# Value tiles loaded by natural rows, weights in 1 KB runs, and a replanned order table, in a local attention with attention experts behind it

## The chip, the cores and the metric

The kernel runs on one core of one Trainium2 chip. The metric is the device time of one execution in microseconds, as the median of several executions. Beside it there is a profile of one execution; its span runs from the first to the last instruction. The engines are named as in the profile: PE is TensorE's matmuls and PEld its weight loads, DVE is VectorE, ACT is ScalarE, POOL is GpSimd, SP is SyncE, which here only issues transfers. ACT issues some transfers too, between its own work. Every engine works through its instructions in order.

## The reference

There are two stages. The first is attention with a local window of 96 keys and 8 global keys, for 4 batches, 8 heads, 768 positions and 64 numbers per head. The second takes the first's output, with the heads side by side (512 numbers per position), through four causal attention experts; a gate picks two of the four for each position.

```python
# first stage: q, k, v are [4, 8, 768, 64] float32
scores = scale * np.matmul(q, k.transpose(0, 1, 3, 2))
rel = pos[:, None] - pos[None, :]
keep = (pos[None, :] < n_global) | ((rel >= 0) & (rel < n_local))
scores = np.where(keep, scores - slopes[h] * dist, -1e9)
a = np.exp(scores - max); a /= a.sum(-1)
attn = np.matmul(a, v)                       # [4, 8, 768, 64]
x = attn.transpose(0, 2, 1, 3).reshape(4, 768, 512)

# second stage: w_gate [512, 4], wq, wk, wv [4, 512, 64], wo [4, 64, 512]
logits = x @ w_gate                          # softmax over the best two of four
for e in range(4):
    q, k, v = x @ wq[e], x @ wk[e], x @ wv[e]
    a = softmax(causal(scale * q @ k.T))
    out += gate_weight[e] * (a @ v @ wo[e])  # [4, 768, 512] float32
```

## The kernel before

The work is cut into 24 units `u`, each a row tile of 128 positions of one batch (six for each batch). For each unit there is a set of small stages, and a long table, `ORDER`, lists the stages in the order in which they are given to the engines. A slot of the table is two letters for the stage, the number of the unit, and a letter for the engine: `g` POOL, `a` ACT, `v` DVE for copies and casts, `s` SP and `a` ACT for transfers. So `lq0s` loads tile 0 of the queries on SP's queue, `qc0g` casts it to 16 bits on POOL, `tk0` and `tq0a` turn keys and queries on PE and copy the result on ACT, `sa0` and `sb0` are tile 0's local scores with their exponential on ACT, `gs` the global scores, `vs` the selected global values, `va` and `vb` the local values, `tx` turns x, `pk`, `pq` and `pv` project it, `ca`, `cb` and `cc` are the causal scores, `ma` their mask on POOL, `za` and `zb` the causal values, `tz` and `ou` the output, `ro` the routing, `wi` and `wc` load and cast weights. `xb`, `xg` and `az` fill constants on DVE.

Keys and queries are loaded by row tile, with the positions on the partitions. For the values, the local stage wants another layout: 64 keys on 64 partitions, heads 0 to 3 on the lower half of the partitions and heads 4 to 7 on the upper half. The kernel before loads them from memory in that layout, so that one cast for each unit is enough:

```python
raw = fast.enter_context(tc.tile_pool(name="raw", bufs=4))

def load(u, nm, on):
    b, ri = divmod(u, NT)
    f = fs[nm, u] = raw.tile([P, H, Dh], F32, name=nm + "f")
    queues[on](f[:, :, :], {"k": k, "q": q}[nm][b, :, ri * P:(ri + 1) * P, :]
               .rearrange("h j d -> j h d"))

def load_v(i, on):
    if i < 2:                                # tiles 0 and 1 of the first batch alone
        parts = [(hf, slice(0, HG), 2 * i + c) for hf in range(2) for c in range(2)]
        b = 0
    else:                                    # one head of each half, all the batch's rows
        b, hq = divmod(i - 2, HG)
        parts = [(hf, hq, slice(0 if b else 4, 2 * NT)) for hf in range(2)]
    if i == 0 or i > HG + 1 and hq == 0:
        fs["v", b] = raw.tile([P, HG, 2 * NT, Dh], F32, name="vf", bufs=2)
    for hf, h, c in parts:
        o, r = fs["v", b][hf * KB:(hf + 1) * KB], v[b, hf * HG:(hf + 1) * HG]
        if i < 2:
            queues[on](o[:, :, c, :], r[:, c * KB:(c + 1) * KB, :].rearrange("h j d -> j h d"))
        else:
            queues[on](o[:, h, c, :], r[h, c.start * KB:c.stop * KB, :]
                       .rearrange("(c j) d -> j c d", j=KB))

def cast_v(u, on):
    b, ri = divmod(u, NT)
    copies[on](take("vbuf", u)[:, :, :, 0:Dh],
               fs["v", b][:, :, 2 * ri:2 * ri + 2, :].rearrange("r h c d -> r c h d"))
```

The weights of keys, queries and values are loaded with position `kp` of 128 on the partition and four chunks `ko` behind each other, which makes pieces of 256 bytes; the gate's weights make pieces of 16 bytes.

```python
def weights_in(i, on):
    w32s[i] = wst.tile([P, E, NK, Hd], F32, name="w32", tag="w32")
    issue = queues[on]
    if i < 3:
        issue(w32s[i][:, :, :, :],
              (moe_wk, moe_wq, moe_wv)[i].rearrange("e (ko kp) d -> kp e ko d", kp=P))
    else:
        ...                                  # wo
    if i == 2:
        w32s["g"] = wst.tile([P, NK, E], F32, name="wg32", tag="wg32", bufs=1)
        issue(w32s["g"][:, :, :], moe_w_gate.rearrange("(ko kp) e -> kp ko e", kp=P))

def turn_x(u, on):
    x_ps = psT.tile([P, NK, P], F16, name="xps", tag="t")
    for j in range(NK):
        nc.tensor.transpose(x_ps[:, j, :],
                            x16s[u][:, j // 2, 2 * (j % 2):2 * (j % 2) + 2, :]
                            .rearrange("r h d -> r (h d)"), ident[:, :])
    xTs[u] = pp.tile([P, NK, P], F16, name="xT")
    copies[on](xTs[u][:, :, :], x_ps[:, :, :])
```

The beginning of its order table:

```
az0 lq0s xb0 lk0s qc0g kc0g tk0 lv0a lk1a vc0g lq1s lk2s kc1g lk3s lq2a lq3s lq4a xg0 tq0a lk4s
tk1 qc1g tq1v wi0a kc2a gi0 kc3v vs0 lv1s sa0 tk2 lq5s qc2g tq2v tk3 lk5a az1 az2 az3 sb0 qc3g
tq3v az4 gs0 vg0 qc4g kc4g lq6s tk4 lv2s wi1a tq4v lk6a sa1 sa2 va0 vb0 sb1 sa3 lv3s kc5v vc1g
lv4s lv5a vg1 va1 vb1 qc5g qc6g sb2 lk7s tk5 tq5v lq7s wc0g wi2a lk8a lk9s tx0v tx1v wc1g kc6v
sa4 sa5 pk0 pk1 lq8s pq0v vc2g vc3v vc4g pq1v vc5g sb3 vg2 gs1 tk6 kc7v lv6s va2 ca0 vb2 lq9a
...
```

Of the kernel before, what the change touches and what calls it, by code (L numbers as in the profile page):

```python
# [22 lines left out]
def kernel(  # L23
# [120 lines left out]
    def weights_in(i, on):  # L144

        w32s[i] = wst.tile([P, E, NK, Hd], F32, name="w32", tag="w32")
        issue = queues[on]
        if i < 3:
            issue(w32s[i][:, :, :, :],
                  (moe_wk, moe_wq, moe_wv)[i].rearrange("e (ko kp) d -> kp e ko d", kp=P))  # L150
        else:
            issue(w32s[i][:, :, :, :].rearrange("p e k d -> p (e k d)")
                  .rearrange("p (a m) -> p a m", a=NEP),
                  moe_wo.rearrange("(a b) d m -> (b d) a m", b=2))
        if i == 2:
            w32s["g"] = wst.tile([P, NK, E], F32, name="wg32", tag="wg32", bufs=1)
            issue(w32s["g"][:, :, :], moe_w_gate.rearrange("(ko kp) e -> kp ko e", kp=P))  # L157

    def weights_cast(i, on):
# [6 lines left out]
        elif i == 2:  # L166
# [3 lines left out]
            copy(wvg16[:, :, E * Hd:E * Hd + E], w32s["g"][:, :, :])  # L170
# [8 lines left out]
    raw = fast.enter_context(tc.tile_pool(name="raw", bufs=4))  # L179
# [8 lines left out]
    NA, NV, NV2 = 5, 8, 2 * NT + 2  # L188
    rings = {}
# [34 lines left out]
    def load(u, nm, on):  # L224
        b, ri = divmod(u, NT)
        f = fs[nm, u] = raw.tile([P, H, Dh], F32, name=nm + "f")
        queues[on](f[:, :, :], {"k": k, "q": q}[nm][b, :, ri * P:(ri + 1) * P, :]
                   .rearrange("h j d -> j h d"))

    def load_v(i, on):  # L230

        if i < 2:
            parts = [(hf, slice(0, HG), 2 * i + c) for hf in range(2) for c in range(2)]
            b = 0
        else:
            b, hq = divmod(i - 2, HG)
            parts = [(hf, hq, slice(0 if b else 4, 2 * NT)) for hf in range(2)]
        if i == 0 or i > HG + 1 and hq == 0:  # L240
            fs["v", b] = raw.tile([P, HG, 2 * NT, Dh], F32, name="vf", bufs=2)
        for hf, h, c in parts:
            o, r = fs["v", b][hf * KB:(hf + 1) * KB], v[b, hf * HG:(hf + 1) * HG]
            if i < 2:
                queues[on](o[:, :, c, :], r[:, c * KB:(c + 1) * KB, :].rearrange("h j d -> j h d"))
            else:
                queues[on](o[:, h, c, :], r[h, c.start * KB:c.stop * KB, :]  # L247
                           .rearrange("(c j) d -> j c d", j=KB))
# [8 lines left out]
    def cast_v(u, on):  # L257
        b, ri = divmod(u, NT)
        copies[on](take("vbuf", u)[:, :, :, 0:Dh],  # L259
                   fs["v", b][:, :, 2 * ri:2 * ri + 2, :].rearrange("r h c d -> r c h d"))  # L260
# [41 lines left out]
    def global_scores(g):  # L302

        u0 = g * NH
        b, r0 = divmod(u0, NT)
        kg = kgs[b]
        g_ps = psS.tile([P, NH * P], F32, name="gps", tag="s")
# [3 lines left out]
        for p in range(NP):  # L311
            for c0, c1 in (((0, P), (P, NH * P)) if r0 == 0 else ((0, NH * P),)):
# [4 lines left out]
        ag = pp.tile([P, NH * P], F16, name="ag", bufs=3)  # L317
        S_.activation(ag[:, :], g_ps[:, :], func=Exp, bias=gbias[:, :], scale=sc1)
        ags[g] = ag
# [29 lines left out]
    def global_values(u):  # L349

        c = (u % NT % NH) * P
        ag, vg = ags[u // NH], vgs[u // NT]
        zs_[u] = psZ.tile([P, 2, 4 * P], F32, name="zps", tag="z")
        for hf in range(2):
            r = slice(hf * Dh, hf * Dh + Dh)
            mm(zs_[u][:, hf, 0:HG * VW].rearrange("r (h d) -> r h d", h=HG),  # L356
               lhsT=ag[r, c:c + P], rhs=vg[r, :, :],
# [25 lines left out]
    def turn_x(u, on):  # L383
        x_ps = psT.tile([P, NK, P], F16, name="xps", tag="t")
        for j in range(NK):
            nc.tensor.transpose(x_ps[:, j, :],  # L386
                                x16s[u][:, j // 2, 2 * (j % 2):2 * (j % 2) + 2, :]
                                .rearrange("r h d -> r (h d)"), ident[:, :])
# [75 lines left out]
    def causal_values(u, i):  # L464
# [4 lines left out]
        if i == 0:  # L469
            zs2[u] = psZ.tile([P, 2, 4 * P], F32, name="zps2", tag="z")  # L470
# [71 lines left out]
    def general_path(ctx):  # L542
# [35 lines left out]

        ident32 = gc.tile([P, P], F32, name="ident32")
# [20 lines left out]
        with tc.For_i(0, B, 1) as b:  # L600
# [43 lines left out]
            for ri in range(NT):  # L644
                l_ps = gp.tile([P, MAXB], F32, name="gs", tag="s", bufs=2)
                for ko in range(NK):
                    mm(l_ps[:, 0:E], lhsT=xT[:, ko, ri * P:(ri + 1) * P],
                       rhs=wvg16[:, ko, E * Hd:E * Hd + E],
# [6 lines left out]
            for e in range(E):  # L655
                for w, dst, nm in ((wq16, qs, "q"), (wk16, ks, "k")):
                    d = gb.tile([Hd, S], F16, name=f"g{nm}T{e}")
                    for c in range(2):
                        p_ps = gp.tile([P, MAXB], F32, name="gs", tag="s", bufs=2)
                        for ko in range(NK):  # L660
                            mm(p_ps[0:Hd, 0:S // 2], lhsT=w[:, ko, e // 2, e % 2, :],
# [6 lines left out]
                for ct in range(NT):  # L668
                    p_ps = gp.tile([P, MAXB], F32, name="gs", tag="s", bufs=2)
                    for ko in range(NK):  # L670
                        mm(p_ps[:, 0:Hd], lhsT=xT[:, ko, ct * P:(ct + 1) * P],
                           rhs=wvg16[:, ko, e * Hd:(e + 1) * Hd],
# [41 lines left out]
        "lk": (load, "k"), "lq": (load, "q"), "lv": (load_v,),  # L714
# [3 lines left out]
        "az": (local_zeros,), "xt": (act_tables,),  # L718
# [40 lines left out]

ORDER = """  # L760
az0 lq0s xb0 lk0s qc0g kc0g tk0 lv0a lk1a vc0g lq1s lk2s kc1g lk3s lq2a lq3s lq4a xg0 tq0a lk4s
tk1 qc1g tq1v wi0a kc2a gi0 kc3v vs0 lv1s sa0 tk2 lq5s qc2g tq2v tk3 lk5a az1 az2 az3 sb0 qc3g
tq3v az4 gs0 vg0 qc4g kc4g lq6s tk4 lv2s wi1a tq4v lk6a sa1 sa2 va0 vb0 sb1 sa3 lv3s kc5v vc1g
lv4s lv5a vg1 va1 vb1 qc5g qc6g sb2 lk7s tk5 tq5v lq7s wc0g wi2a lk8a lk9s tx0v tx1v wc1g kc6v
sa4 sa5 pk0 pk1 lq8s pq0v vc2g vc3v vc4g pq1v vc5g sb3 vg2 gs1 tk6 kc7v lv6s va2 ca0 vb2 lq9a
tq6v sb4 sb5 lk10s lk11a qc7g wc2g tk7 tq7v vg3 va3 tx2v kc8g vb3 kc9v sa6 sb6 lv7s pv0v pv1a
vg4 va4 qc8g qc9g vb4 lv8a lv9s pk2 pq2a tk8 tq8v kc10v lk12s ca1 lk13a vg5 lq10s lq11s va5
tx3v lq12s tk9 tq9v gi1 gs2 tx4v vb5 pv2a pv3a sa7 sa8 tx5v ma0 pk3 ro0 vc6g ro0 vc7v vc8v pq3a
# [68 lines left out]
```

## Time and profile before

| | before |
|---|---|
| time, median of 3 | 161.3 us (161.09 to 161.34) |
| span of the profiled execution | 160.6 us |
| PE busy | 134.7 us (84%) |
| DVE, ACT busy | 112.0 us (70%), 105.4 us (66%) |
| POOL busy | 71.1 us (44%) |
| moved by transfers | 27.80 MB, 173 GB/s over the span |
| packets under 512 B | 82256 of 85623 |

A busy share is an average over the whole span. The page also cuts the span into 40 slices and gives each engine a digit for each slice, in tenths. The chain of waits follows the work that ended last back to the start: at each step, to what released it. The groups of instructions give the count, the busy time and the mean time of one for each line and shape; behind the second bar stands how long the engine stood idle before them and what it waited for.

### The profile page before, as it was taken

How to read it: one execution, taken by the hardware profiler on the slowest of the kernel's cores; microseconds unless marked ns; L12 is line 12 of the kernel's file. 1: busy time of each engine (PE TensorE's matmuls, PEld its weight loads, DVE VectorE, ACT ScalarE, POOL GpSimd, SP SyncE). 2: the span in 40 equal slices, each digit the busy share in tenths (PEclk: the TensorE clock that was granted, in tenths of full speed). 3: DMA queues.
4: the chain of work that ended last, by engine and by line, in shares of the span. 5: the costliest groups of instructions: out<-in, count | busy, mean ns of one | idle time of the engine just before them, and what ended most of it. 6: DMA issues, size and time to landing. Idle time of an engine off the chain costs nothing.

```text
span 160.6 us, 6996 instructions
## 1 busy us (share of the span) xinstructions
PE 134.7 (84%) x2950; PEld 105.8 (66%) x2950; DVE 112.0 (70%) x343; ACT 105.4 (66%) x171; POOL 71.1 (44%) x187
## 2 busy tenths in 40 slices
PE   0266585779999999899999999999999999999710
PEld 0143363758778879787798876887889778776300
DVE  7978424248769977597796588788866788798530
ACT  0283051074648878788968988989878788799520
POOL 4454343093308463976636643603435254633100
PEclk9999558778999999999999999999999999999995
DMA  5999998999999989795499999032100103042550
GB/s 115 273 288 257 260 236 180 270 257 224 241 256 247 255 189 284 169 225 140 126 227 232 228 293 251 33 131 76 65 6 0 69 6 135 0 172 93 200 208 8
DMA packets 85623, 27.80 MB, mean 173 GB/s; under 512 B 82256, under 2 KB 82256, under 8 KB 85584
## 3 DMA queue, kind: packets, MB, share of 16 engines
q1 hardware_dynamic: 64480, 21.63, 53.6%
q10 hardware_dynamic: 21104, 5.65, 15.8%
q8 instruction: 25, 0.41, 1.1%
q14 instruction: 14, 0.11, 0.2%
HBM read 20.98 MB, written 6.29 MB: 170 GB/s over the span
## 4 chain that ended last, share of the span: by engine, by line
PE 60%; DMA 16%; ACTq 5%; SPq 4%; DVE 3%; ACT 2%; issue 2%; POOL 2%; POOLq 0%
DMA vf<-in_v_dram 11%; PE pps L401 11%; PE vps L415 7%; PE cps L446 6%; PE zps L371 6%; PE tp L267 6%; PE zps L474 5%; PE ops L502 4%; PE sps L334 4%; PE xps L386 4%; SPq L247 3%; DMA kf<-in_k_dram 3%; PE sps L341 3%; ACTq L157 3%; PE zps L356 2%; DMA out_dram<-osb 2%
## 5 line engine op out<-in xcount | busy, mean ns | idle before, releaser
L449 ACT ACTIVATE a<-cps 128x1024 f16<-128x1024 f32 (+1 forms) x48 | 42.0, 915 | 5.7 <-PE cps L446 5.1
L344 ACT ACTIVATE abuf<-sps 128x636 f16<-128x636 f32 (+1 forms) x48 | 30.7, 684 | 20.3 <-PE sps L341 8.5
L259 POOL CAST vbuf<-vf 128x512 f16<-128x512 f32 x20 | 12.3, 637 | 20.5 <-DMA vf<-in_v_dram 9.9
L334 PE MATMUL sps<-biasT,ident 64*64 64x318 f16 (+1 forms) x192 | 16.0, 333 | 5.8 <-ACT abuf L344 5.8
L461 POOL TENSOR_SCALAR_AFFINE_SELECT a<-a 128x256 f16<-128x256 f16 x48 | 18.5, 415 | 5.2 <-ACT a L449 5.2
L276 DVE COPY kqT<-tp 128x1024 f16<-128x1024 f16 x22 | 15.0, 685 | 6.1 <-PE tp L267 5.9
L267 PE MATMUL tp<-ident,s16k 128*128 128x128 f16 x96 | 10.5, 239 | 8.6 <-POOL s16k L255 8.1
L380 DVE TENSOR_TENSOR x<-zps,rinv 128x512 f16<-128x512 f32 x24 | 16.6, 691 | 0.8
L255 POOL CAST s16q<-qf 128x512 f16<-128x512 f32 x21 | 12.9, 622 | 8.6 <-DMA qf<-in_q_dram 5.7
L371 PE MATMUL zps<-vbuf,abuf 64*128 64x65 f16 x704 | 16.7, 195 | 0.0
L341 PE MATMUL sps<-kqT 64*64 64x159 f16 (+2 forms) x384 | 15.6, 243 | 0.8 <-issue 0.7
L371 PEld LDWEIGHTS <-abuf 64*128 64x128 f16 x704 | 15.2, 98 | 1.1 <-issue 0.4
L401 PE MATMUL pps<-xT,wk 128*128 128x128 f16 x192 | 15.4, 227 | 0.0
L474 PE MATMUL zps<-v2buf,a 128*128 128x65 f16 x336 | 15.3, 193 | 0.0
L401 PE MATMUL pps<-xT,wq 128*128 128x128 f16 x192 | 14.9, 223 | 0.0
L474 PEld LDWEIGHTS <-a 128*128 128x128 f16 x336 | 12.9, 97 | 1.7 <-DVE zs L485 0.2
L502 PE MATMUL ops<-wo,zt 128*128 128x512 f16 x48 | 13.5, 380 | 0.4 <-DVE zt L495 0.4
L341 PEld LDWEIGHTS <-kqT 64*64 64x64 f16 x384 | 12.3, 116 | 2.4 <-issue 1.4
L415 PE MATMUL vps<-wvg,xT 128*128 128x260 f16 x96 | 13.7, 274 | 0.0
L267 PEld LDWEIGHTS <-s16k 128*128 128x128 f16 x96 | 6.6, 106 | 10.6 <-POOL s16k L255 8.3
L446 PEld LDWEIGHTS <-kq 64*128 64x128 f16 x336 | 9.7, 94 | 4.9 <-issue 3.8
L446 PE MATMUL cps<-kq,kq 64*128 64x128 f16 x240 | 12.9, 217 | 0.0
(111 smaller groups left out, 267.5 us busy)
## 6 DMA issues: line engine op xcount, KB each, us to landing
out_dram<-osb SPq DMA_DIRECT2D x24, 256.0 KB, 2.3
qf<-in_q_dram SPq DMA_DIRECT2D x20, 256.0 KB, 4.8
kf<-in_k_dram SPq DMA_DIRECT2D x18, 256.0 KB, 4.9
vf<-in_v_dram SPq DMA_DIRECT2D x22, 192.0 KB, 4.4
kf<-in_k_dram ACTq DMA_DIRECT2D x6, 256.0 KB, 5.2
qf<-in_q_dram ACTq DMA_DIRECT2D x4, 256.0 KB, 5.3
vf<-in_v_dram SPq DMA_DIRECT2D x6, 128.0 KB, 6.5
w<-in_moe_wk_dram ACTq DMA_DIRECT2D x1, 512.0 KB, 6.7
```

Of the source, the lines that this page charges most:

```text
L267: nc.tensor.transpose(tps[u][:, i, p, :], s16s["kq"[i], u][:, 2 * p:2 * p + 2, :].rearrange("j h d -> j (h d)"), ident[:, :])
L334: mm(s_ps[o, hh, 0:2 * w].rearrange("r (c n) -> r c n", c=2), lhsT=ident2[r, :], rhs=biasT[r, p, 0:w].unsqueeze(1).to_broadcast([KB, 2, w] ...
L341: mm(s_ps[o, hh, c * w:c * w + n], lhsT=kqT[b][r, 0, p, k0:k0 + KB], rhs=kqT[b][r, 1, p, k0:k0 + n], start=False, stop=True, skip_group_ch ...
L344: S_.activation(as_[u][:, :, g, :].rearrange("r h (c n) -> r h c n", c=2)[:, :, :, 0:w], s_ps[:, :, 0:2 * w].rearrange("r h (c n) -> r h c ...
L371: mm(zs_[u][:, hf, hq * VW:(hq + 1) * VW], lhsT=as_[u - prev][r, hq % 2, hq // 2, at:at + P], rhs=held("vbuf", u - prev)[r, c, hq, :], sta ...
L401: mm(p_ps[:, i, ep, :], lhsT=w[:, ko, ep, :, :].rearrange("r a d -> r (a d)"), rhs=xT[:, ko, :], start=(i == 0 and ep == 0 and ko == 0), s ...
L415: mm(v_ps[:, :], lhsT=xT[:, ko, :], rhs=wvg16[:, ko, :], start=(ko == 0), stop=(ko == NK - 1))
L446: mm(s_ps[:, e2, i, :], lhsT=kqs[b * NT + ci][r, 0, ep, :], rhs=kqs[u][r, 1, ep, :], start=(i == 0), stop=True, skip_group_check=True)
L449: S_.activation(a2[:, :, 4 * c:4 * c + len(part), :], s_ps[:, :, 0:len(part), :], func=Exp, scale=sc2)
L461: G.affine_select(out=d, in_=d, pattern=[[0, NEP], [1, P]], channel_multiplier=-1, base=0, compare_op=Alu.is_ge, fill=0.0)
L474: mm(z_ps[:, e, :], lhsT=a2[:, e % 2, (e // 2) * n + ci, :], rhs=held("v2buf", b * NT + ci)[:, e, :], start=(e == 0 and ci == 0), stop=Tru ...
L502: mm(o_ps[:, :], lhsT=zts[u][:, ep, :], rhs=wo16[:, ep, :], start=(ep == 0), stop=(ep == NEP - 1))
```

## The change

The values are loaded as keys and queries are, by row tile with the positions on the partitions, in one transfer of 256 KB for each unit. The cast then does the moving: four casts for each unit, each of 64 partitions and four heads, two of which read one half of the partitions and write the other. That lets the values of a unit arrive when it needs them, and not a quarter of a batch at a time. With six buffers instead of four, loads can run further ahead.

The weights are laid out with four neighbouring rows on one partition, which makes runs of 1 KB (64 bytes for the gate), and x is turned with a stride of four to match. The general path, which the inputs here don't take, loads weights of its own. Global scores are made one unit at a time for the first three units. Matmuls of the identity with itself, which compute nothing that is used, can be put into the order to keep PE busy (`wm`). The order table is a new one, for all of this.

```diff
@@ weights_in
+        issue = queues[on]
+        if i == 4:
+            w32s[i] = wst.tile([P, NK, E], F32, name="wg32", tag="wg32", bufs=1)
+            issue(w32s[i][:, :, :].rearrange("p k e -> p (k e)"),
+                  moe_w_gate.rearrange("(kp ko) e -> kp (ko e)", ko=NK))
+            return
         w32s[i] = wst.tile([P, E, NK, Hd], F32, name="w32", tag="w32")
-        issue = queues[on]
         if i < 3:
-            issue(w32s[i][:, :, :, :],
-                  (moe_wk, moe_wq, moe_wv)[i].rearrange("e (ko kp) d -> kp e ko d", kp=P))
+            issue(w32s[i][:, :, :, :].rearrange("p e k d -> p e (k d)"),
+                  (moe_wk, moe_wq, moe_wv)[i].rearrange("e (kp ko) d -> kp e (ko d)", ko=NK))
@@
-    raw = fast.enter_context(tc.tile_pool(name="raw", bufs=4))
+    raw = fast.enter_context(tc.tile_pool(name="raw", bufs=6))
@@ load; load_v goes
-        queues[on](f[:, :, :], {"k": k, "q": q}[nm][b, :, ri * P:(ri + 1) * P, :]
+        queues[on](f[:, :, :], {"k": k, "q": q, "v": v}[nm][b, :, ri * P:(ri + 1) * P, :]
@@
+    def keep_warm(n):
+        alone = "z" not in current
+        if alone:
+            current["z"] = psZ.tile([P, 2, 4 * P], F32, name="zps", tag="z")
+        for _ in range(n):
+            mm(current["z"][:, 0, 4 * P - 2 * NC:4 * P].rearrange("r (a n) -> r a n", a=2),
+               lhsT=ident[:, :], rhs=ident[:, 0:NC].unsqueeze(1).to_broadcast([P, 2, NC]),
+               start=alone, stop=True, skip_group_check=True)
+            alone = False
@@ cast_v
-        b, ri = divmod(u, NT)
-        copies[on](take("vbuf", u)[:, :, :, 0:Dh],
-                   fs["v", b][:, :, 2 * ri:2 * ri + 2, :].rearrange("r h c d -> r c h d"))
+        o = take("vbuf", u)
+        for hf in range(2):
+            for c in range(2):
+                copies[on](o[hf * KB:(hf + 1) * KB, c, :, 0:Dh],
+                           fs["v", u][c * KB:(c + 1) * KB, hf * HG:(hf + 1) * HG, :])
@@ global_scores
-        u0 = g * NH
+        u0, n = (g, 1) if g < NH else ((g - NH + 1) * NH, NH)
@@ turn_x
-                                x16s[u][:, j // 2, 2 * (j % 2):2 * (j % 2) + 2, :]
-                                .rearrange("r h d -> r (h d)"), ident[:, :])
+                                x16s[u][:, :, :, :].rearrange("r a h d -> r (a h d)")
+                                .rearrange("r (c k) -> r k c", k=NK)[:, j, :], ident[:, :])
@@ ORDER, its first lines
+wi4a lq0s qc0g lk0a kc0g wm17 tk0 lv0a lk1a vc0g lq1s xt0 lk2s xb0 xg0 kc1g lq2a lk3a lq3s lq4s
+qc1g tq0a wm12 vs0 az0 gi0 tk1 tq1v lk4a gs0 wm3 gs1 kc2g lv1s az1 az2 lk5s wm1 sa0 lv2s qc2g
+sb0 kc3v lq5a qc3v qc4g tk2 tq2v tk3 tq3v vg0 wi0s wi1s va0 vb0 az3 az4 kc4g kc5v vc1g gs2 lv3a
+lv4s vc2g sa1 sb1 wc0g tk4 wc1g tq4v vg1 sa2 sb2 lk6s wi2s va1 qc5a vb1 sa3 sb3 tx0v tk5 tq5v
+vg2 va2 vb2 gs3 sa4 tx1v tx2v sb4 lq6a lq7s lk7s lk8s lv5a pk0 pk1 vc3v sa5 vc4g wc2g sb5 lq8s
 ...
```

Of the 24 value casts, the new table gives 23 to POOL and one to DVE; before, 20 were POOL's. Of the 48 casts of keys and queries POOL has 33 (34 before), DVE 12 and ACT 3.

## The prediction

> **What bounds the kernel now.** I read the page first, for where the engines are idle in time and not only on average:
>
> ```profile
> span 160.6 us, 6996 instructions
> ...
> PE 134.7 (84%) x2950; PEld 105.8 (66%) x2950; DVE 112.0 (70%) x343; ACT 105.4 (66%) x171; POOL 71.1 (44%) x187
> ...
> PE   0266585779999999899999999999999999999710
> ...
> PEclk9999558778999999999999999999999999999995
> DMA  5999998999999989795499999032100103042550
> ```
>
> One slice is 4 us. TensorE (PE) is full from the tenth slice until near the end; the holes are in the first nine slices, where the DMA row is full and the clock row drops. So there are three stages: a ramp, a dense stretch, a tail. I cut the span at the changes of the granted clock:
>
> ```profile
> core 0: us, PE busy (x) PEld busy (x) DVE busy (x) ACT busy (x) POOL busy (x), PEclk, DMA share, GB/s
> 5.70:13.40 7.70, 5.17 (x60) 3.60 (x60) 5.86 (x27) 4.35 (x6) 3.33 (x6) 1.00 1.24 280
> ...
> 27.06:30.47 3.41, 3.12 (x37) 3.00 (x37) 0.00 (x0) 0.23 (x1) 0.00 (x0) 0.50 1.23 274
> ...
> 33.89:37.30 3.41, 3.41 (x71) 2.69 (x71) 1.50 (x3) 1.73 (x4) 2.50 (x8) 0.50 1.19 267
> 37.30:147.30 110.00, 108.43 (x2537) 87.08 (x2535) 85.92 (x259) 89.11 (x146) 53.68 (x144) 1.00 0.61 156
> 147.30:160.60 13.30, 5.03 (x64) 2.62 (x62) 4.63 (x20) 4.14 (x8) 0.77 (x2) 0.86 0.35 128
> ```
>
> From 37.3 to 147.3 PE is busy 108.4 of 110 us at full clock: only less PE work shortens it, and the change takes none away. The tail is 13.3 us of last outputs and final checks, which the change hardly touches. What can move is the 37.3 us of ramp. The chain of waits, cut to that ramp, says what it is made of:
>
> ```profile
> 3.60 4.79 DMA kf<-in_k_dram
> ...
> 9.94 6.66 DMA vf<-in_v_dram
> ...
> 19.34 6.59 DMA vf<-in_v_dram
> ...
> 26.67 0.55 ACTq L149
> ...
> 27.26 4.31 ACTq L157
> ...
> 32.18 0.71 ACT abuf L344
> ```
>
> Columns: start, length, what. Two value transfers (13.3 us), one key transfer (4.8 us), and the issue of the gate weights on ScalarE's (ACT) queue: 4.31 us during which the exponential of 32.18 has to wait.
>
> **What the Trainium skill says.**
> 1. "TensorE: Matmul & The Clock Gate", Part 1 (the HAM clock gate): PE runs at half rate until it has been busy for a window of about 3.4 us, and falls back after an idle one. The trace agrees: windows of 3.41 and 6.85 us at 0.50, and eight transposes take 0.60 us of the chain at 37.2 against four taking 0.53 us at 33.9. Before 13.4 us there is no clock record (the page prints 1.00), yet four transposes span 0.61 us there, as in a half-rate window.
> 2. "DMA: Bandwidth & Descriptors", Specifications: runs of at least 512 B are needed for line rate. The trace fits: 82256 of 85623 packets are under 512 B, and with the share above 1 the rate is 250 to 280 GB/s. That 1 KB runs are faster, no row here shows.
> 3. The first of these pages, Weight-path perf modes: a fast weight load takes 32-column chunks "packed or strided". So the new stride of four in the x transposes should leave the load at its 97 ns; no run shows it yet.
> 4. "SBUF — State Buffer", SBUF: two separate sides: VectorE (DVE) and GpSimd (POOL) lock a shared port pair against each other. The trace fits: the DVE cast of a key tile takes 416 to 870 ns.
>
> **The change part by part.**
>
> *Values by row tile.* The 40 issues for the 24 tiles (8 small ones and 32) become 24 of 256 KB, on the natural rows. Tile 0's values no longer take the four ACT issues (2.75 us together) that stood before key tile 1, and a tile's values no longer wait for a quarter of a batch. The moving to halves becomes four casts of 64x256 for each tile. Unit cost:
>
> ```profile
> L259 POOL CAST vbuf<-vf 128x512 f16<-128x512 f32 x20 | 12.3, 637 | 20.5 <-DMA vf<-in_v_dram 9.9 <-DMA qf<-in_q_dram 6.1 <-DMA out_dram<-osb 3.1
> L164 POOL CAST wk<-w 128x256 f16<-128x256 f32 x4 | 1.4, 400 | 0.0
> ```
>
> A cast of 256 columns costs 400 ns whatever it holds; I take the same for 64 partitions, since DVE takes 218 ns for a 159-column cast on 64 partitions and for a 128-column one on 128. The new table gives POOL 23 of 24 tiles: 23 x 4 x 0.40 = 36.8 us for 12.3, so POOL goes from 71 to about 95 us, 63% of a shorter span. PE never waits for the average, only for a late cast or mask.
>
> *Weights.* The gate's 16-byte pieces become one 64-byte run per partition: 4.31 us of issue becomes about 0.4 us at the very start. The other issues move to SyncE's queue. Bytes are the same.
>
> *Order table.* First, the constants on DVE: the selector for the global values ends at 10.2 us now; two zeroings (0.55 us) no longer stand in front, so 9.7. PE does its 17 warm matmuls while tile 0 arrives (16 bits, 240 columns, into a spare PSUM region: no data, 33 in all, at about 0.1 to 0.2 us, so 3.3 to 6.6 us, put where PE has nothing to do). Then, walking the new order with the old durations: selected values copied on ACT 9.9 to 10.7, first global exponentials to 11.7, tile 0's two local ones (0.70 each) to 13.1, its values on PE at about 13.6 (17.5 now). After that ACT sets the pace: eight local exponentials 5.6, two single global ones about 0.7, one query cast 0.62, or 7 us: 21. The first projection also needs key and query weights: ahead of them lie 15 tiles of 0.262 MB, with both weights 5.0 MB; at 270 GB/s from 2 us on they have landed at 20.5 us, and four casts of 0.40 end at 22.1. So projections start at 22 to 23 us instead of 27.9, with more behind them.
>
> Now a *matching point*. At 37.3 us the old program has turned tiles 0 to 6, has local values for 0 to 2 and projections for 0 and 1. The new order has as much PE work done when it has projected tiles 0 and 1 and has the values of tile 3: it lacks one turn and one causal score (0.65 us) and is ahead by a tile's values and an x transpose (1.05 us). From the first projection that is 4 x 0.46 (16 matmuls took 0.89 us) + 0.67 (scores) + 0.75 (values), 3.3 us of PE, some 4 with ACT's two exponentials: 26 to 27. I add 1 for waits I don't see: 27.5.
>
> *Sum.* 27.5 + 110 (same dense work) + 13.3 (tail) = 150.8 span. Two more global-score groups cost about 0.3, the surplus at the matching point gives 0.4 back. For DMA and POOL, both closer to PE than before, I allow 1.0 us of new idle. Span about 151.7; the timed median is 0.7 above the profiled span (161.3 against 160.6): 152.4, rounded to **152.5 us**, 8.8 less.
>
> **The rivals.**
> - *Bandwidth takes the place of issue and order.* Tile 7 needs 7.1 MB: at 270 GB/s it is there at 28.3 us, and PE asks for it at about 31. Tile 15 needs 13.4 MB: 51.6 against 54. Slack of 2 to 3 us. For it: DMA's share is above 1 over most of the ramp. Against it: the dense stretch draws only 156 GB/s. At 245 GB/s the slack is gone and PE waits 2 to 3 us: 155.
> - *GpSimd becomes the bound.* If a partition-moving cast costs 0.8 us and not 0.4, POOL reaches 71 - 12 + 74 = 133 us, its queue is in order, masks and key casts stand behind value casts, and most of the gain goes: 158 to 162. Against it: POOL's own row is 44% now. With 0.4 us it costs 1 to 3 us.
> - *The clock stays low.* If the warm matmuls don't carry PE over, half-rate windows like those at 16.8, 27.1 and 33.9 come back; each of 3.4 us costs up to 1.7: two give 155 to 156.
> - *The early work was hidden anyway.* If the dense stretch had slack, an earlier start would be lost. Against it: 98.6% busy at full clock.
>
> **Range and chances.** The ramp could end at 25.5 (everything meets) or at 31 (bandwidth and a clock window): 150.5 and 156. With tail and dense stretch uncertain by 1 us, 8 in 10 lies in 149.5 to 157.5. Faster by over 2% means under 158.1, which only the GpSimd rival or two rivals together would prevent: 0.85; within 2% 0.11; slower 0.04.
>
> **What would show it.** Right: PE's digits at 9 from the seventh slice instead of the tenth; no half-rate window after about 17 us; projections first at 22 to 23 us; no wait of 4 us on a weight issue; value casts of about 400 ns; POOL near 95 us; the dense stretch still about 110 us and the tail 13. Wrong: value casts at twice that, masks or values as longest releasers of PE in the middle, x weight loads well over 97 ns, or a dense stretch that has grown by what the ramp lost.

## The result, and the profile after

The changed kernel takes 153.9 us (median of four executions, 152.33 to 154.82) where the kernel before takes 161.3. The ratio is 0.949, with a 95% interval of 0.938 to 0.960 (how ratios are taken is said above the table of runs). A second set of six executions on another chip gave 154.4 us and 0.952 (0.946 to 0.958). The page of the profiled execution, cut to the lines shown of before:

```profile
span 151.9 us, 7115 instructions
...
PE 137.3 (90%) x2987; PEld 107.5 (71%) x2987; DVE 111.3 (73%) x343; ACT 105.6 (70%) x174; POOL 94.6 (62%) x258
...
PE   5889969989999998899999999999999999999700
...
PEclk9999999999999999999999999999999999999995
DMA  4999999979899898999994994345013003116540
```

A slice is now 3.8 us. PE's row is at 8 or 9 from the second slice, but for one 6, where the kernel before reached its steady 9 only in the tenth. The clock row has no 5 before the last slice, but it has no record before 14.4 us, and until then PE ran at half rate (the lines are under no_warm); its digits there also count the warm matmuls. Two 8s remain in slices 16 and 17, at 57 to 65 us. The same three stages, cut at the predicted matching point and at the tail:

```profile
core 0: us, PE busy (x) PEld busy (x) DVE busy (x) ACT busy (x) POOL busy (x), PEclk, DMA share, GB/s
0.00:27.90 27.90, 23.63 (x415) 17.16 (x416) 21.11 (x68) 13.50 (x23) 18.84 (x51) 1.00 1.08 261
27.90:139.20 111.30, 109.14 (x2528) 88.12 (x2525) 85.95 (x257) 89.02 (x146) 74.97 (x206) 1.00 0.67 169
139.20:151.90 12.70, 4.51 (x53) 2.26 (x50) 4.24 (x19) 3.06 (x6) 0.77 (x2) 0.83 0.36 132
```

Tiles 0 and 1 are projected, and the projection of tile 2 begins, at 27.9 us. The middle stage has the same amount of PE work as before (109.1 against 108.4 us), and 2.2 us of idle time where before there were 1.6. What the ramp lost is what the kernel gained: 9.4 us less in front, 1.3 more in the middle, 0.6 less in the tail make the 8.7 by which the span is shorter. The chain of waits in the first 40 us, its main entries:

```profile
14.37 6.66 DMA qf<-in_q_dram
21.11 0.62 ACT s16q L250
...
24.79 5.50 DMA qf<-in_q_dram
30.31 0.53 DVE s16q L250
```

Value transfers and the weight issue are gone from it; two query transfers stand there instead. The first is query tile 5, issued on ACT's queue, behind exponentials, at 14.37 only. PE waits 1.24 us for its cast, and the first projection begins at 24.7:

```profile
21.78 0.40 PE L266 MATMUL tp<-ident,s16q 128*128 128x128 f16 x4 [1.24 <-ACT s16q L250]
```

The value casts have their own line among the groups:

```profile
L258 POOL CAST vbuf<-vf 64x256 f16<-64x256 f32 x92 | 37.0, 402 | 6.6 <-DMA vf<-in_v_dram 2.6
```

### The profile page after: what moved, and what is told of

Same layout as the page of the kernel before. It is cut to its first block, busy times and chain, and to the rows that moved or that the text cites. A ratio compares the mean times of both kernels' runs of the same rounds, so it can differ in the third digit from the quotient of the medians.

```text
span 151.9 us, 7115 instructions
## 1 busy us (share of the span) xinstructions
PE 137.3 (90%) x2987; PEld 107.5 (71%) x2987; DVE 111.3 (73%) x343; ACT 105.6 (70%) x174; POOL 94.6 (62%) x258
## 4 chain that ended last, share of the span: by engine, by line
PE 61%; DMA 11%; DVE 9%; POOL 9%; issue 3%; ACT 2%; POOLq 0%; ACTq 0%; DVEq 0%
DMA qf<-in_q_dram 11%; PE pps L401 10%; PE zps L474 7%; PE ops L502 7%; PE vps L415 6%; PE cps L446 6%; PE zps L371 4%; PE sps L335 4%; POOL vbuf L258 4%; PE tp L266 4%; PE xps L386 3%; PE sps L342 3%; PE ztps L491 2%; PE zps L356 2%; POOL s16q L250 1%
## 5 line engine op out<-in xcount | busy, mean ns | idle before, releaser
L258 POOL CAST vbuf<-vf 64x256 f16<-64x256 f32 x92 | 37.0, 402 | 6.6 <-DMA vf<-in_v_dram 2.6
L461 POOL TENSOR_SCALAR_AFFINE_SELECT a<-a 128x256 f16<-128x256 f16 x48 | 18.4, 411 | 12.8 <-ACT a L449 12.8
L275 DVE COPY kqT<-tp 128x1024 f16<-128x1024 f16 x23 | 15.5, 686 | 5.3 <-PE tp L266 5.1
L371 PE MATMUL zps<-vbuf,abuf 64*128 64x65 f16 x704 | 15.2, 189 | 0.0
L335 PE MATMUL sps<-biasT,ident 64*64 64x318 f16 (+1 forms) x192 | 14.8, 313 | 0.1
L401 PE MATMUL pps<-xT,wk 128*128 128x128 f16 x192 | 14.6, 219 | 0.1
L371 PEld LDWEIGHTS <-abuf 64*128 64x128 f16 x704 | 13.9, 94 | 0.6
L342 PE MATMUL sps<-kqT 64*64 64x159 f16 (+2 forms) x384 | 14.2, 228 | 0.0
L415 PE MATMUL vps<-wvg,xT 128*128 128x260 f16 x96 | 13.6, 275 | 0.0
L250 POOL CAST s16k<-kf 128x512 f16<-128x512 f32 x17 | 10.3, 609 | 5.2 <-DMA kf<-in_k_dram 3.3
L401 PEld LDWEIGHTS <-wk 128*128 128x128 f16 x192 | 11.5, 98 | 1.8 <-issue 0.2
L342 PEld LDWEIGHTS <-kqT 64*64 64x64 f16 x384 | 11.4, 108 | 1.1 <-issue 0.2
L401 PEld LDWEIGHTS <-wq 128*128 128x128 f16 x192 | 11.6, 98 | 0.1
```

Of the source, the lines that this page charges most:

```text
L258: copies[on](o[hf * KB:(hf + 1) * KB, c, :, 0:Dh], fs["v", u][c * KB:(c + 1) * KB, hf * HG:(hf + 1) * HG, :])
L335: mm(s_ps[o, hh, 0:2 * w].rearrange("r (c n) -> r c n", c=2), lhsT=ident2[r, :], rhs=biasT[r, p, 0:w].unsqueeze(1).to_broadcast([KB, 2, w] ...
L342: mm(s_ps[o, hh, c * w:c * w + n], lhsT=kqT[b][r, 0, p, k0:k0 + KB], rhs=kqT[b][r, 1, p, k0:k0 + n], start=False, stop=True, skip_group_ch ...
L371: mm(zs_[u][:, hf, hq * VW:(hq + 1) * VW], lhsT=as_[u - prev][r, hq % 2, hq // 2, at:at + P], rhs=held("vbuf", u - prev)[r, c, hq, :], sta ...
L401: mm(p_ps[:, i, ep, :], lhsT=w[:, ko, ep, :, :].rearrange("r a d -> r (a d)"), rhs=xT[:, ko, :], start=(i == 0 and ep == 0 and ko == 0), s ...
L415: mm(v_ps[:, :], lhsT=xT[:, ko, :], rhs=wvg16[:, ko, :], start=(ko == 0), stop=(ko == NK - 1))
```

## The experiments

Each set of runs was made on a chip of its own, beside the kernel before. Times and spans are in us; "first", "tile 10" and "tile 23" are the starts of the key projections of tiles 0, 10 and 23 in the profiled execution; idle is PE's idle time from the projection of tile 2 to that of tile 23. Times are medians of all executions, and ratios leave out those over 1.5% above the fastest of their kernel, so that a ratio need not be the quotient of the two times beside it; where fewer than three were left there is no ratio, the times left are given singly, and a profile that fell in one left out is not read for positions.

The chips are not alike: the median span of the kernel before is 160.5 us beside after_again to no_warm, 159.0 beside one_cast to runs_256, 158.5 beside fewer_bytes to deep, and 160.3 beside deep_no_warm. So between these groups the ratios decide, and a difference of 1 or 2 us in span is not read as one. The stretch from tile 10 to tile 23 takes 59.2 to 59.4 us in every profile with the new order and the new layout that is read here, whatever the chip.

| run | time | before there | ratio, 95% | span | first | tile 10 | tile 23 | idle |
|---|---|---|---|---|---|---|---|---|
| before | 161.3 | | | 160.6 | 27.9 | 78.7 | 142.2 | 1.6 |
| after | 153.9 | 161.3 | 0.949 (0.938–0.960) | 151.9 | 24.7 | 72.6 | 131.9 | 2.0 |
| after_again | 154.4 | 162.3 | 0.952 (0.946–0.958) | 152.8 | 25.0 | 73.2 | 132.6 | 2.2 |
| old_values | 175.7 | 162.3 | 1.085 (1.075–1.095) | 172.2 | 29.5 | 88.9 | 152.6 | 13.0 |
| old_order | 162.4 | 162.3 | – | – | – | – | – | – |
| no_warm | 154.5 | 162.3 | 0.954 (0.947–0.961) | 152.7 | 24.3 | 72.6 | 132.0 | 2.1 |
| one_cast | 153.2, 154.1 | 161.1 | – | 151.4 | 21.7 | 72.3 | 131.5 | 4.1 |
| no_stride | 155.7 | 161.1 | 0.971 (0.958–0.984) | 152.6 | 23.3 | 73.5 | 132.8 | 3.5 |
| gate_16 | 154.1 | 161.1 | – | – | – | – | – | – |
| runs_256 | 154.5 | 161.1 | – | – | – | – | – | – |
| fewer_bytes | 152.2 | 160.6 | 0.952 (0.945–0.959) | 148.8 | 24.3 | 70.0 | 129.3 | 0.3 |
| better | 154.0 | 160.6 | 0.961 (0.954–0.969) | 150.7 | 22.0 | 71.7 | 131.1 | 2.7 |
| deep | 153.2 | 160.6 | 0.956 (0.950–0.962) | 149.5 | 21.6 | 70.8 | 130.0 | 2.6 |
| deep_no_warm | 153.5 | 162.3 | 0.951 (0.942–0.960) | 151.8 | 24.3 | 72.5 | 131.7 | 1.5 |

The time of deep_no_warm is the median of the three left.

**after_again: the changed kernel once more.**

> The changed kernel once more, beside the runs that undo parts of it. All theories: ratio to before 0.945 to 0.955, span 150 to 152.5 us. It gives the spread of the changed kernel: whether its executions differ by 2 us again.

It repeats the first set within half a per cent, with the first projection at 25.0 and tile 10 at 73.2. Spans of its six executions lie between 151.0 and 152.8, so even on one chip a difference of less than about 1 us between two kernels is not read as one in what follows.

**old_values: the new order with the old value layout.** The values come again in the layout with 64 keys on the partitions, a quarter of a batch at a time, with one cast for each unit. The quarter transfers stand at places of the row-tile loads that they replace.

```diff
-    "lv": (load, "v"), ... four casts of 64x256 for each unit
+    "lv": (load_v,),   ... one cast of 128x512, as in the kernel before
 ORDER: lv4s -> lv4s lv5s; lv6a -> lv6a lv7s lv8s lv9s; lv7 to lv11 go; lv12s -> lv10s lv11s; ...
```

> New order, weights and warm matmuls, but the values loaded in the old layout (by head and batch, one cast per tile); tiles 2 to 5 of the first batch can then be cast only when all four heads' transfers have landed. Theory (the values' arrival sets the ramp): tile 2's value cast starts 2 to 4 us later, the ramp's matching point moves from 27.9 to 30-32 us, span 153 to 156, while POOL falls by 20 us to about 75. Rival (order table does it all): within 1 us of the changed kernel. Rival (the four casts on POOL are a burden that the early arrival only just pays): faster than the changed kernel, span under 150.

It is 8.5% slower than the kernel before, and the span of 172.2 is far beyond the 153 to 156 that the theory gave. The ramp is about as expected (tile 2 is projected at 32.9 us); the 13.0 us of idle time come behind it. What PE waits for longest:

```profile
engine line waited for: us in total, times, longest us
PE zps L389 <- POOL vbuf L276: 5.7, 1, 5.7
PE vgps L312 <- POOL vbuf L276: 5.5, 1, 5.5
PE tp L284 <- DVE s16q L270: 4.0, 1, 4.0
```

And the cast behind it, whose own idle time names the transfer:

```profile
L276 POOL CAST vbuf<-vf 128x512 f16<-128x512 f32 x23 | 14.0, 617 | 36.5 <-DMA vf<-in_v_dram 16.6 <-DMA out_dram<-osb 10.6 <-DMA qf<-in_q_dram 9.3
```

POOL has 71.1 us of work instead of 94.6 and still the kernel is 21 us slower than the changed kernel on the same chip: a quarter holds two heads of every tile, so the cast of a tile's values waits until all four quarters of its batch have landed. The new order asks for values earlier than the old layout can bring them, and PE then falls to half rate in four places (at 23, 47, 81 and 115 us):

```profile
PEclk9999965999957999999699999987999999999985
```

My placing of the quarters in the new table is a choice; a better one would lose less.

**old_order: the new layouts with the old order.** Value loads by row tile stand where the old table loads its quarters, the gate's weights follow the value weights, and there are no warm matmuls.

```diff
-        u0, n = (g, 1) if g < NH else ((g - NH + 1) * NH, NH)
+        u0, n = g * NH, NH
 ORDER: the table of the kernel before, with lv6s -> lv6s lv7s; lv7s -> lv8s lv9s; wi2a -> wi2a wi4a; ...
```

> Old order table, with its value slots turned into row tiles (two or one per slot), with the new value layout, the four casts and the new weights. Theory (the old table's chain was value transfers and the gate's issue, both mended by the layout alone): 4.3 us from the gate, 1 to 3 us from values, less 1 for POOL: span 153 to 157, ratio 0.955 to 0.98. Rival (the order table is what brings it): span 159 to 161, ratio 0.99 to 1.0.

The one execution left takes 162.4 us, the kernel before on the same chip 162.3 (median); the other three took 165.6 to 168.1. So no gain is seen of the layouts with the old order, though one execution is thin evidence, and the new order with the old value layout loses 8.5%; together they bring 5%. The value layout is what permits the order.

**no_warm: the 33 warm matmuls left out.**

```diff
-wi4a lq0s qc0g lk0a kc0g wm17 tk0 lv0a ...
+wi4a lq0s qc0g lk0a kc0g tk0 lv0a ...
```

> The changed kernel without its 33 warm matmuls. Theory: the clock rises one window of 3.4 us later and may fall once in the ramp, but the ramp waits mostly for transfers: 0 to 2 us longer. Rival (the clock is a main part of the gain): half-rate windows of 3.4 to 6.8 us come back as in the kernel before, span 154 to 156.

In time nothing moves: 0.954 against 0.952 on the same chip, with the first projection at 24.3 against 25.0. Why is seen in the warm matmuls' own line in the changed kernel:

```profile
L240 PE MATMUL zps<-ident x33: 381/407/408, 1.6 to 12.7; 128*128 128x240 f16 x33
```

The columns are least, median and greatest duration in ns. All 33 run at the same long duration to the last, so the clock had not risen by 12.7 us (in deep, below, where it had, the shortest took 266). The transposes tell the moment: their median is 311 ns before 14.3 us, and from 14.4 on they take 219; in no_warm the step is at 15.3, in the kernel before at 13.6. That this is not the whole account shows in deep_no_warm below.

**one_cast: values cast once for each unit, not moved to the halves.** It leaves out the movement, so heads and keys of a unit meet the wrong probabilities; the amount of other work is the same.

```diff
-        for hf in range(2):
-            for c in range(2):
-                copies[on](o[hf * KB:(hf + 1) * KB, c, :, 0:Dh],
-                           fs["v", u][c * KB:(c + 1) * KB, hf * HG:(hf + 1) * HG, :])
+        copies[on](o[:, :, :, 0:Dh],
+                   fs["v", u][:, :, :].rearrange("r (c h) d -> r c h d", c=2))
```

> The changed kernel with one straight cast of 128x512 per value tile in place of the four: the move to the halves is left out, so the sums are of the wrong rows, but all else is the same. Theory (POOL has room): POOL falls by 20 us to about 74, the span by 0 to 1 us. Rival (POOL's in-order queue delays masks and casts): the span falls by 2 us or more, and PE's idle time after 28 us goes to nothing.

POOL has 71.6 us of work instead of 94.6, and the time is no different (153.2 and 154.1 us). Its ramp is 3 us shorter, but at tile 10 it is only 0.3 us ahead: 2.1 us reappear as idle time of PE (4.1 us instead of 2.0). Nor is the shorter ramp the casts' doing as far as this shows, since the clock was full from 10.2 us in this profile and from 14.4 in the changed kernel's. The 23 us added to POOL therefore cost nothing that is measured, and something other than POOL decides when tile 10 is projected.

**no_stride: x turned without the stride of four.** Rows of x then meet the wrong rows of the weights; the work is the same.

```diff
-                                .rearrange("r (c k) -> r k c", k=NK)[:, j, :], ident[:, :])
+                                .rearrange("r (k c) -> r k c", k=NK)[:, j, :], ident[:, :])
```

> The changed kernel with x turned in neighbouring columns again, so that x's rows no longer match the weights' rows (numbers are left wrong, shapes and counts are the same). Theory (a strided weight load costs 15 ns more, 113 for 98): loads back at 98 ns, span 0.5 to 1.5 us shorter, as 96 x 15 ns = 1.4 us. Rival (loads run beside matmuls): loads back at 98 ns, span the same within 0.3.

The weight loads of x fall back from 113 to 98 ns, and from tile 10 to tile 23 it takes 59.3 us, the same as with the stride. In time it is not faster (155.7 us); its clock fell back to half rate from 12.1 to 15.5 us. The 15 ns a load are real, and no time is seen to come from them.

**gate_16: the gate's weights in 16-byte pieces again,** but at the new place, first on ACT's queue. Rows then lie in the old order, so the gate's sums differ.

```diff
-            issue(w32s[i][:, :, :].rearrange("p k e -> p (k e)"),
-                  moe_w_gate.rearrange("(kp ko) e -> kp (ko e)", ko=NK))
+            issue(w32s[i][:, :, :], moe_w_gate.rearrange("(ko kp) e -> kp ko e", kp=P))
```

> The changed kernel with the gate's weights in 16-byte pieces again, in the same first place of ACT's queue (rows then don't match x's, numbers are left wrong). Theory (the issue holds the queue): the issue takes 4.3 us instead of 0.43, key tile 0, value tile 0 and key tile 1 come 3.9 us later, the whole span is 3 to 4 us longer. Rival (other transfers take the bandwidth meanwhile, and the ramp is bound by bytes): 0 to 1 us.

The timeline of ACT's queue in gate_16 (start, length, instruction), then the same transfer in the kernel before, then in old_order, where it stands behind the value weights too, but in 64-byte runs:

```profile
0.80 0.48 ACTq L149 DMA_DIRECT2D wg<-in_moe_w_gate_dram  x1
1.31 0.67 ACTq L229 DMA_DIRECT2D kf<-in_k_dram  x1
```

```profile
26.67 0.55 ACTq L149 DMA_DIRECT2D w<-in_moe_wv_dram  x1
27.26 4.31 ACTq L157 DMA_DIRECT2D wg<-in_moe_w_gate_dram  x1
```

```profile
22.43 0.37 ACTq L154 DMA_DIRECT2D w<-in_moe_wv_dram  x1
23.22 0.35 ACTq L149 DMA_DIRECT2D wg<-in_moe_w_gate_dram  x1
```

512 pieces of 16 bytes take 0.48 us to issue when nothing is queued before them, 0.43 us as 128 runs. Behind the 512 KB of the value weights the 128 runs take 0.35 us. So neither the small pieces nor the place makes 4.31 us alone: it took 512 small pieces behind value weights that were themselves in 256-byte pieces, and which of these decides was not separated. Nor is the end of this wait seen to bring time by itself: in old_order it is gone too, and no gain is seen there. The one execution of gate_16 left took 154.1 us, the other three 156.7 to 156.9, so nothing is shown of its time.

**runs_256: each of the three weights by four issues of 256-byte runs.**

```diff
-            issue(w32s[i][:, :, :, :].rearrange("p e k d -> p e (k d)"), ...)
+            for ko in range(NK):
+                issue(w32s[i][:, :, ko, :], ...[:, :, ko, :])
```

> The changed kernel with each of the key, query and value weights loaded by four issues of 256-byte runs instead of one of 1 KB runs; the layout on chip is the same. Theory (run length is a small part): SP's queue spends 9 more issues, the weights land 1 us later at most, span 0 to 1 us longer. Rival (1 KB runs are a main part): query weights land 2 us later or more, the first projection moves from 24.7 to 26.5, span 2 us longer.

The one execution left took 154.5 us, the other three 157.2 to 160.4. The runs do move faster: in the changed kernel the rate from 14.4 to 18.0 us, when weights arrive, is 358 GB/s, against 288 GB/s in the 5.4 us before, when only 256-byte pieces move. In runs_256 the rate in the later stretch is 286 (third line).

```profile
9.00:14.40 5.40, 4.83 (x57) 2.85 (x56) 4.11 (x13) 2.04 (x5) 3.23 (x6) 1.00 1.28 288
14.40:18.00 3.60, 3.53 (x88) 2.78 (x90) 2.94 (x7) 2.39 (x5) 2.62 (x7) 1.00 1.14 358
```

```profile
14.40:18.00 3.60, 3.01 (x82) 2.11 (x80) 3.06 (x9) 2.63 (x5) 2.71 (x6) 1.00 1.27 286
```

But the first projection waits for query tile 5 and not for weights, so the faster runs show no gain of their own. With one execution left, a gain of the runs is not excluded.

So far no single part is seen to change the time, and all variants with the new value layout and the new order reach tile 10 at 72 to 74 us whatever their ramp. The next three runs ask what holds that point.

**fewer_bytes: value tiles 6 to 23 not loaded.** 4.7 MB of 27.8 are left out; the casts read the first six tiles again, so the sums are those of other values.

```diff
+        if nm == "v" and u >= 6:
+            fs[nm, u] = fs[nm, u % 6]
+            return
```

> The changed kernel, with value tiles 6 to 23 not loaded (18 transfers of 262 KB, 4.7 MB of 27.8, left out): the casts read the six tiles loaded first again, so the output is that of other values. Theory (from the first projections to about 70 us the arrival of tiles sets the pace, and all variants so far reach the projection of tile 10 at 72 to 75 us whatever their ramp): PE's idle time between tile 2's and tile 23's projections falls from 2.0 us to under 1, tile 10 is projected at 69 to 71 instead of 72.6, and the span is 2 to 3 us shorter, 149 to 150. Rival (the order of work and the engines' own time set that stretch, and arrival has slack): tile 10 stays at 72 to 73 and the span within 0.7 us of 151.9.

The theory's numbers are met: tile 10 at 70.0, PE idle for 0.3 us, a span of 148.8. From 28 to 70 us in the changed kernel, then in fewer_bytes:

```profile
28.00:70.00 42.00, 39.98 (x957) 32.98 (x956) 32.00 (x89) 31.51 (x54) 29.83 (x75) 1.00 1.00 230
```

```profile
28.00:70.00 42.00, 41.73 (x999) 34.31 (x997) 33.40 (x91) 34.05 (x57) 32.70 (x81) 1.00 0.82 192
```

With fewer bytes PE does 1.75 us more work in the same 42 us, and its idle time there falls from 2.0 to 0.3 us. So the arrival of tiles binds this stretch, by about 2 us; better and deep, on the same chip and with all bytes, idle for 2.7 and 2.6 us. Leaving 18 transfers out frees bandwidth and places in the queues at once, and which of the two counts was not separated. In time no gain over the changed kernel is shown: both have a ratio of 0.952. The ramp is as long as before (24.3), although the clock rises by 10 us here: its chain has query tile 5 on ACT's queue again.

```profile
12.79 7.90 DMA qf<-in_q_dram
20.76 0.62 ACT s16q L253
```

**better: three weight buffers, and query tile 5 on SP's queue.** In the changed kernel SP, which issues in order, stands 4.9 us before the value weights, since the two buffers hold key and query weights until they are cast.

```diff
-    wst = fast.enter_context(tc.tile_pool(name="wst", bufs=2))
+    wst = fast.enter_context(tc.tile_pool(name="wst", bufs=3))
-sb0 kc3v lq5a qc3v qc4g tk2 tq2v tk3 tq3v vg0 wi0s wi1s ...
+sb0 kc3v qc3v qc4g tk2 tq2v tk3 tq3v vg0 lq5s wi0s wi1s ...
```

> The changed kernel with three buffers for the loaded weights instead of two, and query tile 5 loaded on SP's queue ahead of the weights instead of on ACT's behind its exponentials. Theory (the ramp is now held by query tile 5 and by SP, which stands 4.9 us for a weight buffer): PE's wait of 1.2 us for query tile 5 goes, the first projection starts at 23 to 23.7 instead of 24.7, SP's wait for the cast of key weights goes, and the span is 0.5 to 1.5 us shorter. Rival (bytes bound the stretch to 70 us, whatever the ramp): the first projection is earlier, but tile 10 is projected at 72 to 73 as before and the span is within 0.5 us.

SP's waits from 10 to 27 us, the two longest in the changed kernel, then all in better:

```profile
SPq L154 <- POOL wq L166: 3.8, 1, 3.8
SPq L154 <- DMA w<-in_moe_wk_dram: 1.1, 1, 1.1
```

```profile
SPq L230 <- DVE rinv L378: 2.6, 1, 2.6
SPq L230 <- POOL vbuf L258: 2.0, 2, 1.3
SPq L230 <- POOL wvg L172: 1.7, 1, 1.7
SPq L230 <- POOL wq L166: 1.2, 1, 1.2
```

The stand of weight issues (L154) is gone, but SP now stands at tile loads (L230) instead, 7.5 us in all. The first projection starts at 22.0, 2.7 us earlier. Tile 10 is projected at 71.7, only 0.9 earlier: two thirds of the gain are given back before it, as the rival says. The profiled span is 1.2 us shorter, but it comes from another chip, and its clock was full from 6.5 us, so neither that nor the earlier projection can be put down to the edit. In time no gain is shown (0.961 against 0.952).

**deep: also eight buffers for keys and queries and seven for values.**

```diff
-        f = fs[nm, u] = raw.tile([P, H, Dh], F32, name=nm + "f")
+        f = fs[nm, u] = raw.tile([P, H, Dh], F32, name=nm + "f", bufs=7 if nm == "v" else 8)
```

> As the run before it (three weight buffers, query tile 5 on SP's queue), and eight buffers each for loaded keys and queries and seven for values, where the changed kernel has six. Theory (between 30 and 65 us SP stands for buffers to come free, so the 16 DMA engines have holes while PE is about to need tiles): SP's waits on casts nearly vanish, the DMA share between 30 and 60 us rises from 0.85-1.1 to about 1.2, tile 10 is projected at 69 to 71, and the span is 2 to 3 us shorter than the changed kernel's. Rival (the stretch is bound by something else than arrival, or the bytes just collide earlier): tile 10 at 72 to 73, span within 0.7 us of the run before it.

The profile has the numbers that the theory asks for, but not by its mechanism. Tile 10 is at 70.8 and the span is 149.5; its executions have spans of 149.5 to 150.8, against 150.7 to 153.3 for better on the same chip. Over the changed kernel no gain is shown (0.956 against 0.952). And DMA's share did not rise to 1.2:

```profile
30.00:45.00 15.00, 14.93 (x344) 12.22 (x346) 11.74 (x33) 12.01 (x21) 12.95 (x35) 1.00 1.11 250
45.00:60.00 15.00, 14.02 (x364) 11.69 (x365) 10.80 (x34) 11.76 (x20) 10.40 (x26) 1.00 0.97 217
```

From 30 to 45 us it rises from 1.02 to 1.11, from 45 to 60 it stays at 0.97, and PE still idles for 2.6 us. Of the 1.8 us by which tile 10 is earlier than in the changed kernel, none comes from the stretch between the first projection and tile 10, which has become 1.3 us longer (49.2 against 47.9). SP still stands at tile loads for 15.5 us between 28 and 66 us (15.3 in the changed kernel), so more buffers alone don't end that. What would end it was not tried.

**deep_no_warm: deep without its warm matmuls.** The shorter spans of better and deep come with less of a shorter time than they should, so I compared time and span in every execution.

> The run before it (three weight buffers, eight, eight and seven raw buffers, query tile 5 on SP's queue), without its 33 warm matmuls. In every execution so far of a kernel without them the time is 1.68 to 1.81 us above the span; in every one with them it is 1.86 to 3.45 above. Theory (the warm matmuls bring nothing inside the span and cost about 1 us outside it): the time is 1.7 us above the span in every execution, the first projection is within 0.5 us of 21.6, the span is 149.5 to 151, and the time 151.2 to 152.7 against 153.2. Rival (the larger gap belongs to the new order or to a shorter span, and one kernel without warm matmuls was chance): the gap is 2.5 to 3.3 us as with them. Second rival (warm matmuls do keep TensorE's clock up in the ramp): half-rate windows before 25 us, first projection at 23 or later, the span 1 us or more longer.

The time is 1.67 to 1.78 us above the span in all six executions. In all, 56 executions without warm matmuls (those of the kernel before, old_order, no_warm and this one) have a gap of 1.66 to 1.81 us; the 46 with them have 1.86 to 3.45. One run took them out of the changed kernel and one out of deep, with the same result; in old_values, which has them and a long span, the gap is 2.5 to 3.1. So the theory is right about the gap. About the ramp the second rival is right in these two profiles. The transposes from 9 to 18.2 us in deep, then in deep_no_warm:

```profile
L266 PE MATMUL tp<-ident,s16k x16: 219/219/230, 9.8 to 15.4; 128*128 128x128 f16 x16
```

```profile
L266 PE MATMUL tp<-ident,s16k x16: 286/311/314, 10.4 to 18.0; 128*128 128x128 f16 x16
```

With warm matmuls the clock is full by 9.8 us, without them from 18.3 on, and the first projection comes at 21.6 and at 24.3. The spans, 149.5 and 151.8, don't show it, since the kernel before differs by 1.8 us between the two chips. On one chip, after_again and no_warm have median spans of 151.9 and 152.8 and median gaps of 2.5 and 1.7: what the warm matmuls gain inside the span, the gap takes back.

The first projection is thus held by two things beside each other: the clock, and the landing of query tile 5. Where the clock stayed full from 14.4 us or earlier, it starts 3.6 to 4.4 us after the tile has landed:

| | clock seen full by | tile 5 landed | first projection |
|---|---|---|---|
| after | 14.4 | 21.0 | 24.7 |
| fewer_bytes | 10.1 | 20.7 | 24.3 |
| one_cast | 10.2 | 17.9 | 21.7 |
| better | 6.5 | 17.6 | 22.0 |
| deep | 9.8 | 17.7 | 21.6 |
| deep_no_warm | 18.3 | 16.8 | 24.3 |

fewer_bytes has the early clock and the late tile, deep_no_warm the early tile and the late clock, and neither gains. The queue alone does not make the tile late: one_cast has it on ACT's queue as well, issued at 12.6 us, and it landed after 5.2 us, where in fewer_bytes it took 7.9 from 12.8 on. Why, these runs don't show. In time the ratios of deep and deep_no_warm (0.956 and 0.951) can't be told apart. No version here is shown to be faster than the changed kernel.

## Why the prediction was right, by its own steps

- *The sum.* Matching point 27.5, measured 27.9; dense stretch 110 and 1.0 of new idle, measured 111.3 with 0.6 more idle than before; tail 13.3, measured 12.7; span 151.7, measured 151.9. The mechanism, a ramp shortened by about 10 us in front of an unchanged stretch, is shown by these cuts. That it needs layout and order together is supported from the other side by old_values and old_order, which have part of the change each and no gain. How the parts share the ramp is not shown.
- *The mis-sized term* is the last: "the timed median is 0.7 above the profiled span (161.3 against 160.6)". These numbers are from different executions; the profiled one itself took 162.3, so its gap was 1.7. With warm matmuls in the kernel it became 2.0 to 2.8. That covers the 1.4 us between 152.5 and 153.9.
- *First projection at 22 to 23:* measured 24.7. I walked ACT and the weights and overlooked query tile 5, whose transfer I left on ACT's queue behind the exponentials. With it on SP's queue and the clock full early, 22.0 and 21.6 were measured; with an early clock and the tile landing early on ACT's queue, 21.7 (one_cast). The matching point came out right by luck in part: the first projection was about 2 us late, but I had allowed 1 us for waits not seen and 0.7 for ACT behind it, and neither was needed there: from the first projection it took 3.2 us.
- *Gate issue 4.31 to about 0.4:* the number was right (0.43), the reason only half. The pieces make it long only behind other transfers: in the new place they take 0.48 us, and the longer runs take 0.35 behind the value weights (gate_16).
- *Value casts at 0.40 and POOL at about 95:* 0.402 and 94.6. The GpSimd rival would have needed casts of twice that; one_cast shows no cost even of the 23 us added. The ground for 0.40, casts on DVE, was another engine's.
- *The bandwidth rival* was right in kind: PE idles for 2.0 us between 28 and 70 us at 230 GB/s, and loses that idle time when bytes are left out (fewer_bytes). I had put its cost at 2 to 3 us beyond an allowance of 1.0; the dense stretch has 0.6 us more idle time than before, so it stayed inside the allowance. Whether bandwidth or the queues make it is open.
- *Clock.* As predicted, no half-rate window after about 17 us, but not thanks to the warm matmuls in this execution: no_warm has none either after 15.3. I put them at 0.1 to 0.2 us each; they took 0.41 each at half rate.
- *x weight loads at 97 ns:* 113. The lines for the loads of x, before and after:

```profile
L386 PEld LDWEIGHTS <-x x96: 95/98/99, 24.1 to 135.4; 128*128 128x128 f16 x96
```

```profile
L386 PEld LDWEIGHTS <-x x96: 110/113/135, 19.9 to 126.0; 128*128 128x128 f16 x96
```

The Trainium skill, "TensorE: Matmul & The Clock Gate", Weight-path perf modes, has the fast load take strided chunks as well as packed ones. That both cost the same it does not say; I read that into it. A stride of four 16-bit numbers costs 15 ns a load here, and no_stride shows no time lost by it.

## What to carry to other kernels

A change of layout and a change of order can each show no gain and together be worth 5%, so try them together before dropping either. When taking one wait away shows nothing, look for a second that ends at the same moment, and take both away in one run before calling either harmless. A long issue is a question about two things together, what stands before it in the queue and into how many pieces the transfers are cut. A term that joins a profiled span to a timed median should be taken from one and the same execution.

## What the runs showed of the hardware

- Warm matmuls go with about 1 us more between the span and the time (1.86 to 3.45 against 1.66 to 1.81). What happens there the trace doesn't show; it stays open.
- The moment at which the clock rises differs by far more between runs of nearly the same program than I expected: in the ten profiled executions of kernels with the same warm matmuls, the first transposes at the full rate come between 6.1 and 14.4 us, in eight of them by 10.7; in before, no_warm and deep_no_warm, which have none, they come at 13.6, 15.3 and 18.3. The Trainium skill, "TensorE: Matmul & The Clock Gate", Part 1 (the HAM clock gate), says that the window runs freely, and for matmuls back to back it puts the variation of the transition at 0.5 us either way. PE had gaps here, so the runs don't test that figure; they show that it can't be carried over to a ramp with gaps. PE was busy for 4.83 of the 5.40 us before 14.4 in the changed kernel, and still at half rate.
- Runs of 1 KB among 256-byte pieces raise the rate from 288 to 358 GB/s, with a lower DMA share (1.14 against 1.28). Without them it is 286 in the same stretch (runs_256).
